# Fewer dummy matmuls in front, a layer norm's bias moved to VectorE, and a re-found instruction order

## The chip, the cores and the metric

The kernel runs on one core of one Trainium2 chip. The metric is the device time of one execution in microseconds (us). Beside the times there is one profiled execution, with a record of every instruction on five engines: TensorE (PE; PEld are its weight loads), VectorE (DVE), ScalarE (ACT), GpSimd (POOL) and SyncE (SP), which issues most DMAs.

## The reference, cut to what matters

```python
x = A_q                                             # [1, 2048, 512], bfloat16
xn = (x - mean(x)) / sqrt(var(x) + 1e-5)            # layer norm over the last axis
# branch A: a shift convolution (4 taps) of k, times v, then a long convolution over the sequence
k_shift = sum_t k_pad[:, t:t+S, :] * shift_k[:, 3 - t]
kv = k_shift * v
y = irfft(rfft(kv, 2S) * rfft(ssm_k, 2S))[:S] + kv * ssm_D
s = xn * y
# branch B: a gated feed-forward network, 512 -> 1792 -> 512
g = silu((gelu(xn @ w_gate) * (xn @ w_up)) @ w_down)
out = x + s * g
```

## The kernel before, in words

All 2048 rows are held as 16 tiles of 128 x 512 (`X`, normalized in `XN`), in four quarters q of four tiles. Branch B takes each quarter: layer norm (`ln`), transposition to `xnT`, then for each of 14 units (`unit`) gate and up matmuls (four of 128x512 each; the first two units of q 0 in halves of 256), gelu on ScalarE (`GE`), the product on VectorE (`HT`), and the down projection with `Wd` (`down`). Branch A does the long convolution as a two-stage Fourier transform by matmuls. Stage 1 of ssm_k (`stage1("H")`, line 938) writes eight results, which ScalarE evicts into four buffers that lie in unused halves of `XN` and `X`; VectorE adds two halves (line 947), and ScalarE's queue stores each to DRAM as `ZH`. A buffer is free again when its store has landed. They are loaded back as `BH` for stage 2 (32x512 matmuls, line 1010). k and v go the same way (`kshift` on VectorE, lines 987 to 995; `ZK`, `BK`); the product of the spectra (`spectrum`), the inverse (`ZI`, `BI`) and the last stage (line 1248) follow.

All loads go through SyncE's queue, in the order of `ORDER`. The stores of `ZH` and `ZI` are issued by ScalarE, the rest by SyncE.

Every piece of work is a task with one or two engines that can do it, its estimated duration, and the buffers that it reads and writes. `SEQ` lists all tasks by number, in the order in which they are recorded; a "b" behind a number takes the second engine. `Sched.run` goes through that list, and gives buffers and PSUM banks out as they come free by its estimates, so the order and the estimates together set which buffer each task gets. The engines then run their own instructions strictly in the recorded order, with semaphores between them.

`warm_up` (line 684) records `N_WARM` matmuls of a zeroed tile ahead of all others. In `ln` each tile's mean and variance are found on VectorE (lines 832 and 833), the epsilon is added on VectorE (line 840), and GpSimd takes the power -0.5 (line 841). For q > 0 it also makes the bias that ScalarE's form of the norm needs (line 850), in two instructions (lines 845 and 846); VectorE's form of the norm (line 851) needs none. For q = 0 all this is done tile by tile, for the others once for four tiles.

The matmuls of all weights come from one helper (line 626), and many evictions from another (lines 617 to 620).

Of the kernel before, what the change touches and what calls it, by code (L numbers as in the profile page):

```python
# [7 lines left out]
FP32 = mybir.dt.float32  # L8
# [16 lines left out]
N_WARM = 18  # L25
ORDER = "x00 h0 x01 w0 D0 h1 w1 x1 h2 h3 s0 k0 w2 k1 k2 w3 d0 d1 v0 v1 k3 v2 v3 x2 x3"
SEQ = (
# [263 lines left out]
class Sched:  # L291
# [11 lines left out]
    SHARED, WAIT, TAKEN = 46000.0, 3300.0, 1400.0  # L303
# [43 lines left out]
    def run(self):  # L347
# [4 lines left out]
        for name in SEQ.split():  # L352
# [3 lines left out]
            for d in t.deps:  # L356
                base = max(base, d.end + d.lat + (self.SEM if not d.nbytes else (400.0 if d.eng == "loads" else self.HEDGE) if t.opts[0][0] == "PE" else self.SEM if d.eng == "loads" else self.HEDGE2))
# [12 lines left out]
            elif t.nbytes:  # L370
# [5 lines left out]
                if en < self.SHARED:  # L376
                    pipe = max(pipe, en + 1000.0) + t.nbytes / self.SHARE_BW
                    t.end = pipe + 1000.0 + self.WAIT
                else:
                    pipe = max(pipe, t.start + 780.0) + t.nbytes / self.DMA_BW  # L380
                    t.end = pipe + 760.0
# [22 lines left out]
def build_kernel(nc, A_q, A_k, A_v, A_shift_k, A_ssm_k, A_ssm_D, B_w_gate, B_w_up, B_w_down, out):  # L404
    with ExitStack() as es0:
# [262 lines left out]
        def pool_id():  # L668
            P(lambda h: h.memset(NHALF[:], -0.5), [R_nh])
            P(lambda h: h.tensor_scalar(ident[:], K32[:], 0.0, None, ALU.is_equal), [R_id], [R_K32])  # L670
# [664 lines left out]
```

## Time and profile before

| | us |
|---|---|
| median of 3 runs | 191.64 (191.61 to 192.41) |
| the profiled execution | 192.79 |
| its span, first to last record | 191.0 |
| TensorE busy | 184.2 (96%) |
| VectorE busy | 166.0 (87%) |
| ScalarE busy | 139.4 (73%) |
| GpSimd busy | 14.9 (8%) |

Busy times overlap between engines, and within TensorE successive matmuls overlap too, so a high busy share does not by itself say that an engine is the limit. The chain of waits is the page's answer to that: it goes back from the last instruction, at each step to what released it. A row of the timeline gives start, duration of the merged group, engine, line, operation and tiles, and in brackets the idle time ahead of it and what ended that.

### The profile page before, as it was taken

The page shows a single profiled execution, that of the slowest core. Times are in us where ns is not written, and L with a number is a line of the kernel's source. Part 1 is how long each engine was busy: PE and PEld are TensorE (multiplying, and loading weights), DVE is VectorE, ACT ScalarE, POOL GpSimd, SP SyncE. Part 2 cuts the span into 40 slices and gives each one's busy share as a digit, 9 for nine tenths or more (in the row PEclk, how much of TensorE's full clock was granted, in tenths as well). Part 3 has the DMA queues.
Part 4 walks back from the last instruction along what each step waited for, and adds up shares of the span by engine and source line. Part 5 has one row for each costly group of instructions (what it writes and reads, how often), then busy time and mean ns, then how long its engine had stood idle before and what let it go on. Part 6 is the DMA issues. An engine that isn't in the chain of part 4 may idle for free.

```text
span 191.0 us, 3537 instructions
## 1 busy us (share of the span) xinstructions
PE 184.2 (96%) x1381; PEld 79.7 (42%) x1392; DVE 166.0 (87%) x244; ACT 139.4 (73%) x188; POOL 14.9 (8%) x31
## 2 busy tenths in 40 slices
PE   7899999999999999999999999999999999999993
PEld 2576544444333343344443434334343444444442
DVE  6889999999899999998697999979889965448955
ACT  5457999883969677888799678878987644364752
POOL 5310940000000000032000000000000000000000
PEclk9999999999999999999999999999999999999999
DMA  5999999996969964676999996865821355935653
GB/s 172 330 383 331 355 373 374 403 404 126 317 258 287 272 204 178 228 257 213 341 250 238 319 309 228 277 246 203 286 91 58 110 168 169 375 106 189 262 220 110
DMA packets 36422, 47.84 MB, mean 250 GB/s; under 512 B 7347, under 2 KB 26039, under 8 KB 36406
## 3 DMA queue, kind: packets, MB, share of 16 engines
q1 hardware_dynamic: 29878, 39.23, 63.5%
q10 hardware_dynamic: 6528, 8.39, 12.5%
q8 instruction: 11, 0.18, 0.4%
q14 instruction: 5, 0.04, 0.1%
HBM read 27.39 MB, written 14.68 MB: 220 GB/s over the span
## 4 chain that ended last, share of the span: by engine, by line
PE 84%; DVE 11%; issue 2%; ACT 1%; ACTq 0%; DVEq 0%
PE psall L626 72%; PE psall L1010 5%; PE psall L930 2%; PE psall L1248 2%; DVE HT L1178 2%; DVE KAC L993 2%; DVE KTM L991 2%; DVE stats L832 1%; DVE KAC L987 1%; PE psall L938 1%; PE psall L896 1%; ACT GE L1175 1%; DVE HTr L620 1%; PE psall L872 1%; DVE XN L947 1%
## 5 line engine op out<-in xcount | busy, mean ns | idle before, releaser
L626 PE MATMUL psall<-xnT,Wu 128*128 128x512 bf16 (+1 forms) x232 | 55.7, 372 | 0.1
L626 PE MATMUL psall<-xnT,Wg 128*128 128x512 bf16 (+1 forms) x232 | 54.7, 372 | 0.7 <-ACT xnT L617 0.7
L626 PE MATMUL psall<-Wd,HT 128*128 128x512 bf16 (+2 forms) x227 | 51.0, 366 | 1.0 <-issue 0.8
L1178 DVE TENSOR_TENSOR HT<-psall,GE 128x512 bf16<-128x512 f32 x54 | 36.6, 682 | 6.4 <-PE psall L626 5.9
L1175 ACT ACTIVATE GE<-psall 128x512 bf16<-128x512 f32 x54 | 31.5, 607 | 10.4 <-PE psall L626 8.7
L626 PEld LDWEIGHTS psall<-Wd,HT 128*128 128x128 bf16 x238 | 21.5, 98 | 27.7 <-issue 4.6
L626 PEld LDWEIGHTS psall<-xnT,Wg 128*128 128x128 bf16 x232 | 21.5, 98 | 27.5 <-issue 2.1
L626 PEld LDWEIGHTS psall<-xnT,Wu 128*128 128x128 bf16 x232 | 21.4, 98 | 26.5 <-issue 3.0
L617 ACT ACTIVATE BO<-psall 128x1024 bf16<-128x1024 f32 x22 | 21.6, 1025 | 10.3 <-PE psall L1248 5.2
L1113 DVE TENSOR_TENSOR HSW<-KB,HSW 128x2048 bf16<-128x2048 bf16 x16 | 19.2, 1219 | 0.2
L617 ACT ACTIVATE AST<-psall 128x1024 bf16<-128x1024 f32 x14 | 14.3, 1024 | 4.7 <-PE psall L930 2.8
L617 ACT ACTIVATE HSW<-psall 128x1024 bf16<-128x1024 f32 x15 | 14.8, 1023 | 3.2 <-PE psall L1010 3.0
L617 ACT ACTIVATE KB<-psall 128x1024 bf16<-128x1024 f32 x14 | 13.9, 1038 | 2.7 <-PE psall L1010 2.7
L993 DVE TENSOR_TENSOR KAC<-KAC,KTM 128x2048 bf16<-128x2048 bf16 x12 | 14.5, 1212 | 0.0
L991 DVE TENSOR_TENSOR KTM<-KK,SKB 128x2048 bf16<-128x2048 bf16 x12 | 14.5, 1212 | 0.0
L1204 DVE SCALAR_TENSOR_TENSOR G<-G,psall 128x512 bf16<-128x512 bf16 x12 | 8.1, 682 | 4.1 <-ACT G L1202 4.1
L832 DVE BATCH_NORM_STATS2 stats<-X 128x6 f32<-128x512 bf16 x16 | 10.5, 681 | 0.7 <-DMA X<-in_A_q_dram 0.7
L617 ACT ACTIVATE XN<-psall 128x1024 bf16<-128x1024 f32 x10 | 10.2, 1023 | 1.1 <-PE psall L938 1.1
L841 POOL TENSOR_TENSOR mv<-mv,NHALF 128x1 f32<-128x1 f32 (+1 forms) x7 | 5.8, 828 | 66.0 <-DVE mv L840 66.0
L1136 DVE TENSOR_TENSOR HSW<-HSW 128x2048 bf16<-128x2048 bf16 x8 | 9.7, 1217 | 0.0
L1113 DVE TENSOR_TENSOR KB<-KB,HSW 128x2048 bf16<-128x2048 bf16 x8 | 9.6, 1217 | 0.0
L1202 ACT ACTIVATE G<-psall 128x512 bf16<-128x512 f32 x12 | 7.0, 596 | 3.2 <-PE psall L626 2.9
(85 smaller groups left out, 155.6 us busy)
## 6 DMA issues: line engine op xcount, KB each, us to landing
BH<-ZH SPq DMA_DIRECT2D x8, 512.0 KB, 5.4
HSW<-HSW SPq DMA_DIRECT2D x16, 256.0 KB, 4.3
BK<-ZK SPq DMA_DIRECT2D x8, 512.0 KB, 5.1
ZI<-BO ACTq DMA_DIRECT2D x16, 256.0 KB, 2.5
BI<-ZI SPq DMA_DIRECT2D x8, 512.0 KB, 4.6
ZK<-AST SPq DMA_DIRECT2D x7, 512.0 KB, 2.9
ZH<-XN ACTq DMA_DIRECT2D x5, 512.0 KB, 3.8
Hn<-in_A_ssm_k_dram SPq DMA_DIRECT2D x4, 512.0 KB, 7.4
```

The costliest lines, as they stand in the source:

```text
L617: return h.activation(o, i, ACTF.Copy, scale=scale)
L626: return h.matmul(o, lhsT=l, rhs=r, start=st, stop=sp)
L832: t_stats[t] = op([("DVE", 670.0)], lambda e, h, t=t: h.bn_stats(stats[:, t, :], X[:, t, :]), r=[bX[q][t % 4]], w=[bst[t]], rr=[R_X[t]], w ...
L991: op([("DVE", dur)], lambda e, h, j=j, m=m: h.tensor_tensor(KTM[:, m.slot, :, :], kk(j), sk(j), ALU.mult), r=need + [bSKB[j], a], w=[m], r ...
L993: op([("DVE", dur)], lambda e, h, m=m: h.tensor_tensor(KAC[:, a.slot, :, :], KAC[:, a.slot, :, :], KTM[:, m.slot, :, :], ALU.add), r=[m], ...
L1010: trk.op("PE", lambda h: h.matmul(ps(s, i)[b, :], lhsT=wt(col)[a, :], rhs=data(col)[a, :], start=n < 16, stop=n >= len(todo) - 16, tile_po ...
L1113: return hd.tensor_tensor(pair(KB, *(2 * DM * z for z in slots())) if to else x, k, x, ALU.mult)
L1136: return hd.tensor_tensor(x, x, y, ALU.add)
L1175: op([("ACT", act(512))], lambda e, h: h.activation(GE[:, g.slot, :], bank(pg), ACTF.Gelu_apprx_tanh), r=[pg], w=[g], rr=lambda: R_bank(pg ...
L1178: op([("DVE", dve(512, 1))], lambda e, h: h.tensor_tensor(HT[:, q % 2, m, :], bank(pu), GE[:, g.slot, :], ALU.mult), r=[pu, g], w=[bHT[q][m]],
L1202: op([("ACT", act(n))], lambda e, h, g=g, pc=pc: h.activation(g, pc(), ACTF.Tanh, scale=0.5), r=[p], w=[bt], rr=lambda p=p: R_bank(p), ww= ...
L1204: op([("DVE", dve(512, 1))], lambda e, h, g=g, pc=pc: h.scalar_tensor_tensor(out=g, in0=g, scalar=1.0, in1=pc(), op0=ALU.add, op1=ALU.mult ...
```

## The change

- `N_WARM` is 12 in place of 18.
- For q > 0 the bias is one VectorE instruction (mean x -1 x rstd) in place of a multiply and a negation on GpSimd. For q = 0 the epsilon may also be added by ScalarE, with a new constant tile `EPSC`; the new `SEQ` does so for two of the four tiles.
- The estimates in `Sched.run` are changed: a task of TensorE that depends on another of TensorE starts at that one's end without a margin; a store that begins between 31 and 46 us is taken to land behind the last load; the power for q > 0 is taken to last 2.5 us in place of 0.85, and ten of the dummies to run at 427 ns in place of seven.
- `SEQ` is new throughout. In the built program the first matmuls behind the dummies are both halves of ssm_k's first tile, then two tiles of `XN`; the first three ZH stores follow each other directly, the next three as well; and the last down projection ends with all fourteen 384-wide matmuls and then all fourteen 128-wide ones, where before four of the 128-wide ones came ahead of the last five of the 384-wide. The number of matmuls is otherwise the same.

```diff
-N_WARM = 18
+N_WARM = 12
...
 SEQ = (
-    "16 17 18 19 20 0 2 7 21 8 4 6 3 10 11 22 23 1 24 25 26 27 65 66 73 67 68 76 28 48 5 74 75 86 49 9 12 90 71 77 29 30 78 87 31 32 33 34 35 36 37 "
...
+    "2 3 16 0 7 17 18 19 20 21 1 10 8 22 9 11 23 24 25 65 66 12 4 6 48 67 26 5 73b 49 68 76 74 75 86 90 77 78 87 71 91b 27 28 29 30 72 82 83 69 70 "
...
-    SHARED, WAIT, TAKEN = 46000.0, 3300.0, 1400.0
+    EARLY, SHARED, WAIT, TAKEN = 31000.0, 46000.0, 3300.0, 1400.0
...
-                if en < self.SHARED:
+                if en < self.EARLY:
                     pipe = max(pipe, en + 1000.0) + t.nbytes / self.SHARE_BW
                     t.end = pipe + 1000.0 + self.WAIT
+                elif en < self.SHARED:
+                    pipe = max(pipe, t.start + 780.0) + t.nbytes / self.DMA_BW
+                    t.end = max(pipe + 760.0, 200.0 + max(l.end for l in order if l.eng == "loads"))
...
+            P(lambda h: h.memset(EPSC[:], LN_EPS), [R_ep])
...
-        t_warm = S.add([("PE", 7 * 427.0 + (N_WARM - 7) * 217.0)], warm_up, r=[bwarm], w=[warm])
+        t_warm = S.add([("PE", 10 * 427.0 + (N_WARM - 10) * 217.0)], warm_up, r=[bwarm], w=[warm])
...
-                t_var = op([("DVE", 180.0)], lambda e, hd, ts=ts: hd.tensor_scalar(mv[:, ts, 2:3], mv[:, ts, 1:2], LN_EPS, None, ALU.add), r=bm, w=[be], rr=rm, ww=rm)
-                t_pw = op([("POOL", 850.0 if q else 600.0)], lambda e, hd, ts=ts, n=n: hd.tensor_tensor(mv[:, ts, 3:4], mv[:, ts, 2:3], NHALF[:, 0:n, :], ALU.pow),
+                def var(e, hd, ts=ts):
+                    if e == "ACT":
+                        return hd.activation(mv[:, ts, 2:3], mv[:, ts, 1:2], ACTF.Identity, bias=EPSC[:, 0, :], scale=1.0)
+                    return hd.tensor_scalar(mv[:, ts, 2:3], mv[:, ts, 1:2], LN_EPS, None, ALU.add)
+                t_var = op([("DVE", 180.0)] + ([] if q else [("ACT", 240.0)]), var, r=[bconst, *bm], w=[be], rr=rm + [R_ep], ww=rm)
+                t_pw = op([("POOL", 2500.0 if q else 600.0)], lambda e, hd, ts=ts, n=n: hd.tensor_tensor(mv[:, ts, 3:4], mv[:, ts, 2:3], NHALF[:, 0:n, :], ALU.pow),
                           r=[bconst, be] + bm, w=[b], rr=rm + [R_nh], ww=rm)
                 bn = B(f"nb{q}_{h}")
                 if q:
-                    op([("POOL", 800.0)], lambda e, hd, ts=ts: hd.tensor_tensor(NB_[:, ts, :], mv[:, ts, 0:1], mv[:, ts, 3:4], ALU.mult), r=[b], w=[bn], rr=rm, ww=R_nb[ts])
-                    op([("POOL", 500.0)], lambda e, hd, ts=ts: hd.tensor_scalar(NB_[:, ts, :], NB_[:, ts, :], -1.0, None, ALU.mult), r=[bn], w=[bn], rr=R_nb[ts], ww=R_nb[ts])
+                    op([("DVE", 200.0)], lambda e, hd, ts=ts: hd.scalar_tensor_tensor(out=NB_[:, ts, :], in0=mv[:, ts, 0:1], scalar=-1.0, in1=mv[:, ts, 3:4], op0=ALU.mult, op1=ALU.mult), r=[b], w=[bn], rr=rm, ww=R_nb[ts])
```

More of the change, by code (lines that the diff above doesn't have):

```diff
@@ L356, in run @@
             for d in t.deps:
-                base = max(base, d.end + d.lat + (self.SEM if not d.nbytes else (400.0 if d.eng == "loads" else self.HEDGE) if t.opts[0][0] == "PE" else self.SEM if d.eng == "loads" else self.HEDGE2))
+                base = max(base, d.end if d.eng == "PE" == t.opts[0][0] else d.end + d.lat + (self.SEM if not d.nbytes else (400.0 if d.eng == "loads" else self.HEDGE) if t.opts[0][0] == "PE" else self.SEM if d.eng == "loads" else self.HEDGE2))
             for b in t.w:
@@ L440, in build_kernel @@
         NHALF = new("NHALF", [128, 4, 1], FP32)
+        EPSC = new("EPSC", [128, 1, 1], FP32)
         NB_ = new("NB_", [128, NT, 1], FP32)
@@ L530, in build_kernel @@
         R_nh = res("NHALF", NHALF[:])
+        R_ep = res("EPSC", EPSC[:])
         R_nb = [res(f"nb{t}", NB_[:, t, :]) for t in range(NT)]
```

41 rows, old and new, of the table SEQ are left out of this document.

## The prediction

> **What bounds the kernel now.** I read the page first, then the chain of waits, then the busy time by stretches.
>
> ```profile
> span 191.0 us, 3537 instructions
> ...
> PE 184.2 (96%) x1381; PEld 79.7 (42%) x1392; DVE 166.0 (87%) x244; ACT 139.4 (73%) x188; POOL 14.9 (8%) x31
> ...
> PE 84%; DVE 11%; issue 2%; ACT 1%; ACTq 0%; DVEq 0%
> ```
>
> TensorE is busy 184.2 of 191.0 us and carries 84% of the chain that ended last; VectorE carries 11%. So the time is the sum of TensorE's instructions plus the few places where it stands still, and only what shortens that sum or those places counts. The profiled execution took 192.79 us with this span of 191.0; the median of the three timed runs is 191.64. I carry differences from the span over to the median.
>
> ```profile
> 14.94 2.39 DVE stats L832 x4
> ...
> 36.65 2.76 PE psall L626 x12
> ...
> 156.68 11.82 PE psall L626 x54
> ```
> ```profile
> 20.00:30.00 10.00, 10.00 (x55) 4.57 (x52) 10.00 (x15) 9.97 (x14) 5.80 (x6) 1.00 1.07 366
> 30.00:40.00 10.00, 9.95 (x56) 3.92 (x55) 10.00 (x13) 8.90 (x14) 0.00 (x0) 1.00 1.06 397
> ```
>
> The first fence has pieces of the chain (start, us), the second the busy time by stretch: TensorE, weight loads, VectorE, ScalarE, GpSimd. From 14.94 to 36.65 nearly all pieces are VectorE's, which is busy 10.00 of 10.00 us twice running; TensorE has work there too, but cannot get ahead of VectorE. After 36.65 the chain is nearly all TensorE's. The 54 matmuls in 11.82 us give 0.219 us each.
>
> **The dummies and the front.** These rows of the timeline (start, us, engine, line) are the start of the kernel.
>
> ```profile
> 1.21 6.33 PE L626 MATMUL psall<-AST 128*128 128x512 bf16 x18 [1.21 <-DVE AST L680]
> ...
> 4.15 0.69 DVE L832 BATCH_NORM_STATS2 stats<-X 128x6 f32<-128x512 bf16 x1 [0.19 <-DMA X<-in_A_q_dram]
> ...
> 5.40 0.57 POOL L841 TENSOR_TENSOR mv<-mv,NHALF 128x1 f32<-128x1 f32 x1 [1.90 <-DVE mv L840]
> ...
> 5.71 0.20 ACT L732 ACTIVATE COLS<-COLS 128x1 f32<-128x1 f32 x1
> ...
> 6.17 0.40 DVE L851 TENSOR_SCALAR XN<-X,mv 128x512 bf16<-128x512 bf16 x1
> ...
> 7.04 0.69 DVE L832 BATCH_NORM_STATS2 stats<-X 128x6 f32<-128x512 bf16 x1 [0.46 <-DMA X<-in_A_q_dram]
> ...
> 7.37 0.61 PE L896 MATMUL psall<-ident,Hn 128*128 128x128 f32 x4
> ...
> 7.82 0.39 PE L872 MATMUL psall<-ident,XN 128*128 128x128 bf16 x4
> ...
> 8.04 0.66 PE L896 MATMUL psall<-ident,Hn 128*128 128x128 f32 x4
> 8.24 1.32 ACT L617 ACTIVATE xnT<-psall 128x512 bf16<-128x512 bf16 x2 [2.33 <-PE psall L872]
> ...
> 9.61 0.61 PE L626 MATMUL psall<-xnT,Wg 128*128 128x256 bf16 x4 [0.69 <-ACT xnT L617]
> ...
> 10.93 0.61 PE L872 MATMUL psall<-ident,XN 128*128 128x128 bf16 x8
> ...
> 13.19 2.75 PE L626 MATMUL psall<-xnT,Wg 128*128 128x512 bf16 x12
> ```
>
> Six dummies of 0.219 us are 1.31 us, so TensorE is free at 7.37 - 1.31 = 6.06. The first tile of ssm_k lies between the two halves of x in the same queue, so it lands between 4.15 and 7.04 (no row has its landing; I take "before 6.06", and lose up to 1.0 us of the gain if not). The new order puts both its halves first: eight transposes of (7.82 - 7.37) / 4 = 0.11 us, until 6.95. Then TensorE needs normalized rows. That chain starts at 4.15 whatever the dummies do, and the change makes its first link later: the variance's epsilon goes from VectorE (0.15 us, line 840) to ScalarE, which is free only after the 5.71 row, at about 5.9. With 0.2 us for it the power begins near 6.2, not 5.40; norm follows 0.2 us after the power's end (5.40 + 0.57 to 6.17), so near 7.0; the transposes come at 7.3 to 7.5 and the second tile's 0.6 later. One eviction is now VectorE's, behind a statistics instruction of 0.69, so both are done by 8.6 to 9.0 instead of 9.61 less the wake-up. The second half of x (7.04) gets its statistics after the norms, so the third and fourth transposes come near 10.4 and 11.5, and TensorE idles before both, which it did not in the one batch at 10.93. After eight more ssm_k transposes it reaches the first 512-wide gate matmuls at 12.4 to 12.8 instead of 13.19, with four more transposes done (0.44 us) and eight fewer 256-wide matmuls of (10.93 - 9.61) / 12 = 0.11 us (0.88 us). Net gain: 13.19 - 12.4 + 0.44 - 0.88 = 0.35 at best by this chain, nothing at 12.8. I take 0.2, with bounds of 0 and, if no wait of the chain were left, 1.31 + 0.69 = 2.0. What covered the removed dummies was thus mostly waiting for x, and that waiting stays.
>
> The granted clock is the second thing that the dummies do: 18 in 6.33 us is far more than 18 x 0.219 = 3.9 us, so (6.33 - 3.94) / 0.219 = about 11 of them ran at half speed. Twelve end about when full speed came. The Trainium skill, "TensorE: Matmul & The Clock Gate", section "Part 1: The HAM clock gate", says that the clock is released after a busy window of about 3.4 us that runs freely, and falls back after an idle window as long; by it the release may come earlier or later from run to run, and the front's gaps, each under 1 us, would not undo it. The trace agrees in part: full speed came some 4.8 us after the first dummy (11 x 0.43), and behind the 0.69 us gap at 9.61 the matmuls still take 0.11 each. The same page, section "A second HAM failure mode: psum-queue depth-cycling", says that frequent short idling can let the clock swing; that is a rival below.
>
> **The late stores.** This is where TensorE stands still in the body.
>
> ```profile
> 36.08 0.37 ACTq L599 DMA_DIRECT2D ZH<-X  x1
> ...
> 43.02 0.61 PE L938 MATMUL psall<-HTr,F 64*128 64x512 bf16 x4
> 43.56 1.90 PE L626 MATMUL psall<-xnT,Wg 128*128 128x512 bf16 x8
> ...
> 46.51 2.08 ACT L617 ACTIVATE X<-psall 128x1024 bf16<-128x1024 f32 x2 [2.98 <-DMA ZH<-X]
> ...
> 49.28 0.39 PE L938 MATMUL psall<-HTr,F 64*128 64x512 bf16 x1
> ...
> 50.11 0.60 PE L938 MATMUL psall<-HTr,F 64*128 64x512 bf16 x3 [0.45 <-ACT GE L1175]
> ```
> ```profile
> ZH<-XN ACTq DMA_DIRECT2D x5, 512.0 KB, 3.8
> ```
>
> The store issued at 36.08 landed at about 46.5, over 10 us later, against a median of 3.8 for its kind: loads were ahead of it. ScalarE stood 2.98 us for its buffer, the gelu evictions queued behind, and TensorE, which wanted their PSUM bank, started the rest of a group at 50.11 that began at 49.28: 0.83 us, where an undisturbed group (43.02 to 43.56) takes 0.54 in all. In the new order three stores stand in a row early, and the fourth stands behind the second quarter's xnT evictions, with two more. Those evictions ran just before the 43.02 row, so these stores fall near the end of the loads; the 46.51 row shows when those were done. Between the fourth store's issue and the eviction that needs its buffer ScalarE has two more issues (0.37 each), a gelu (0.6) and an XN eviction (1.0): 2.3 us. With 3.8 us to land it waits 1.5. In the trace 2.98 cost 0.83, so 2.15 would have cost nothing: 0.83 comes back, with 0.65 to spare. Bounds: the whole 0.83, and far below nothing if the store is slow (the rival).
>
> **The bias.** Three times, GpSimd's multiply and negation become one VectorE instruction.
>
> ```profile
> 22.05 1.02 POOL L841 TENSOR_TENSOR mv<-mv,NHALF 128x4 f32<-128x4 f32 x1
> ...
> 23.15 2.49 POOL L845 TENSOR_TENSOR NB__68<-mv 128x4 f32<-128x4 f32 x1
> ...
> 25.73 0.24 POOL L846 TENSOR_SCALAR NB__68<-NB__68 128x4 f32<-128x4 f32 x1
> ...
> 89.73 1.03 POOL L841 TENSOR_TENSOR mv<-mv,NHALF 128x4 f32<-128x4 f32 x1 [4.07 <-DVE mv L840]
> ```
> ```profile
> L840 DVE TENSOR_SCALAR mv<-mv 128x4 f32<-128x4 f32 x3 | 0.6, 202 | 0.0
> L850 ACT ACTIVATE XN<-X,NB__68,mv x9: 803/819/873, 29.0 to 97.7; 128x512 bf16<-128x512 bf16 x9
> 90.00:100.00 10.00, 9.81 (x87) 4.08 (x88) 8.37 (x9) 8.51 (x11) 1.19 (x3) 1.00 1.05 300
> ```
> GpSimd is done at 25.97, and ScalarE's first norm that reads the bias stands at 29.0, so the 2.7 us that GpSimd saves release nobody. VectorE gets an instruction like the 0.202 us one of line 840. The one for the second quarter of x falls into the stretch where VectorE is full, so it costs its 0.1 to 0.2 us on the path; the others fall where VectorE has 1.6 us free in ten. The instruction waits for the power: in the second quarter nine VectorE instructions stand between, in the last none, so there VectorE stops for about 1.03 + 0.3 us, with the norms and a KB eviction behind it. TensorE is then in matmuls of Wd whose inputs are long made; without that cover it would cost up to 1.3 us.
>
> **The rest of the order and the end.** Counted in the order of the two builds, there are the same matmuls and the same 44 groups of tiled ones among the full ones, so TensorE's sum is otherwise unchanged.
>
> ```profile
> 182.78 5.00 PE L626 MATMUL psall<-Wd,HT 128*128 128x512 bf16 x34
> ...
> 187.27 0.84 ACT L1210 ACTIVATE G<-psall 128x384 bf16<-128x384 f32 x2 [0.44 <-PE psall L626]
> ...
> 188.71 0.23 DVE L1213 TENSOR_TENSOR G<-G,X 128x128 bf16<-128x128 bf16 x1
> ```
> ScalarE's eviction at 187.27 starts a chain that ends the kernel: VectorE works off the 384 columns before the last 128. Now all fourteen 128-wide matmuls stand behind the last 384-wide one, before only ten, so the 384 columns are ready 4 x 0.219 / 4 = 0.2 us earlier against TensorE's end: 0.2 us gained (0 to 0.3). New small waits on a full VectorE between 20 and 50 us no row of before can show; I allow 0.2 in all, the bias's share included (0 to 2).
>
> Sum: -0.2 (front) - 0.83 (store) - 0.2 (end) + 0.2 = -1.03: span 190.0, profiled execution 191.8, median 191.64 - 1.03 = **190.6**. A measurement of this kernel can tell about 0.5%, 0.96 us, from no change; the forecast lies just beyond it.
>
> **Rivals.** *VectorE keeps what is won.* It is full from 14.94 to 36.65, and its first piece there waits for x's next load, not for TensorE. Then the front's gain is gone, the re-found order has small waits of its own in place of the 0.83, and only the end's 0.2 is left: about 191.4. For it: the two rows of 10.00. Against: the 0.83 lies after that stretch. Chance 0.33.
>
> *ScalarE waits for the fourth store.* Its place is the X eviction behind the three stores near 45 us. It decides from a landing of 2.3 + 2.15 = 4.45 us: each us more is a us of TensorE. Half way between 3.8 and the 10.4 of the trace, 7.1, it loses 2.65: 193.25. At 6.45 us the time is 192.6, slower by 0.5%. For it: three stores share the queue, and the loads may end later, since three stores now go early. Against: it is issued when the loads are nearly done. Chance 0.20.
>
> *The clock.* With twelve dummies and gaps behind them full speed comes late or is lost until about 12 us. TensorE's work from 6.06 to 12.4 is 16 transposes of ssm_k and 16 matmuls of 0.11 each and 16 transposes of x of (8.04 - 7.82) / 4 = 0.055, together 4.4 us; at half speed 4.4 more, of which about 2.0 disappear in the gaps: 190.6 + 2.4 = 193.0. Against it: the gaps are short. Chance 0.05.
>
> **How the numbers follow.** The forecast has 0.42: 190.6, and down to 191.64 - 2.0 = 189.6 if the front's waits vanish. So faster 0.42; within 0.5% 0.33; slower 0.20 + 0.05 = 0.25. The forecast's own range is 189.8 to 190.7. The range for 8 in 10 takes in the first rival, the clock and the store up to a landing of 7.05 us: 189.8 to 193.2 leaves out about 0.05 below and 0.12 above.
>
> **What would show it.** Right: the first eight transposes near 6.1, first gate matmuls before 9.1, first 512-wide ones at 12.4 to 12.8; none of the eight groups of ssm_k's first stage (line 938, now 946) over 0.6 us; ScalarE's wait for a ZH store under 2.15 us; the last VectorE row 0.2 us closer to TensorE's end. Wrong: a TensorE gap of over 0.5 us between 40 and 60, a ZH store of over 5 us issued after 44, dummies or transposes at half speed behind 6.1, or VectorE idle behind the power while TensorE waits for it.

## The result, and the profile after

The changed kernel takes 191.03 us (median of seven runs, six of them 190.94 to 191.25). Two disturbed runs, one of 475.59 here and one of 196.06 of the kernel with the third store late, are left out of the ratios; the medians hold all runs. The kernel before, run beside it on the same chip, took 192.3 (191.47 to 193.03). The ratio is 0.994 (95% interval 0.9915 to 0.9965), that is 0.6% or 1.15 us faster. As the control of a later group it gave 191.40 and a ratio of 0.9955 (0.9932 to 0.9978). The forecast was a fall of 1.03 us or 0.54%, between the two. The forecast's 190.6 itself lies 0.4 to 0.8 us below the medians: it stood on a median of three runs for the kernel before, and in the five groups here that kernel has medians of 191.94 to 192.36 and single runs from 191.25 to 193.81. That spread turns out to be half of the story.

The page of the profiled execution (190.94 us), first lines and the shares of the chain of waits:

```profile
span 189.1 us, 3534 instructions
...
PE 183.5 (97%) x1386; PEld 78.4 (41%) x1386; DVE 168.4 (89%) x250; ACT 136.1 (72%) x185; POOL 12.7 (7%) x26
...
PE 92%; DVE 3%; ACT 2%; POOL 1%; issue 0%
```

By the two pages TensorE's busy time is 0.7 us less than before, the span 1.9 us. That does not mean that most of the fall is standing still that went. The page before has 1381 matmuls to 1392 weight loads, this one 1386 of each, so eleven matmul records of before are missing. They are all of the down projection (its group before, then after):

```profile
L626 PE MATMUL psall<-Wd,HT 128*128 128x512 bf16 (+2 forms) x227 | 51.0, 366 | 1.0 <-issue 0.8
L630 PE MATMUL psall<-Wd,HT 128*128 128x512 bf16 (+2 forms) x238 | 51.6, 367 | 0.0
```

Each missing record leaves a gap of 0.05 to 0.16 us that looks like idle time, 1.2 us in all. With them TensorE was busy for about 185.4 us before, and its busy time fell by about as much as the span; the dummies alone last 4.17 us in place of 6.33. TensorE now carries 92% of the chain where it carried 84%; VectorE's 11% became 3%. Of these 1.9 us, 0.7 to 1.0 are this pair of executions (192.79 and 190.94, where the two ratios give 0.9 to 1.15). TensorE's rows of the timeline at the front (start, us, engine, line):

```profile
1.21 4.17 PE L630 MATMUL psall<-AST 128*128 128x512 bf16 x12 [1.21 <-DVE AST L685]
5.55 1.14 PE L904 MATMUL psall<-ident,Hn 128*128 128x128 f32 x8 [0.17 <-DMA Hn<-in_A_ssm_k_dram]
6.70 0.93 PE L880 MATMUL psall<-ident,XN 128*128 128x128 bf16 x8
8.15 1.05 PE L630 MATMUL psall<-xnT,Wg 128*128 128x256 bf16 x8 [0.53 <-DVE xnT L624]
...
12.18 2.11 PE L630 MATMUL psall<-xnT,Wg 128*128 128x512 bf16 x11
```

The dummies are done by 5.4, TensorE then waits 0.17 us for ssm_k's first tile, and the first 512-wide gate matmul stands at 12.18, ahead of the forecast's 12.4 to 12.8. Around the late stores (first three rows ScalarE's queue and ScalarE, then TensorE, then the busy time by stretch in the columns of the prediction's second fence):

```profile
28.40 0.52 ACTq L603 DMA_DIRECT2D ZH<-XN  x1
...
43.95 0.37 ACTq L603 DMA_DIRECT2D ZH<-X  x1
...
48.25 2.08 ACT L621 ACTIVATE X<-psall 128x1024 bf16<-128x1024 f32 x2 [0.92 <-PE psall L946]
```
```profile
47.61 0.61 PE L946 MATMUL psall<-HTr,F 64*128 64x512 bf16 x4
```
```profile
20.00:30.00 10.00, 10.00 (x53) 4.40 (x51) 10.00 (x19) 8.64 (x11) 4.58 (x4) 1.00 1.07 365
30.00:40.00 10.00, 10.00 (x54) 3.88 (x53) 10.00 (x12) 9.94 (x16) 0.00 (x0) 1.00 1.07 400
40.00:50.00 10.00, 10.00 (x59) 4.39 (x58) 10.00 (x13) 7.58 (x10) 0.00 (x0) 1.00 1.06 337
```

The third ZH store is issued at 28.40 where before it was at 36.08, and the fourth at 43.95 landed within 3.9 us. The eviction that needs its buffer (48.25) waited for TensorE, not for a store. The sixth store, issued at 44.88, took 5.5 us, which the prediction names as a sign of being wrong; nothing waited for it. No group of ssm_k's first stage is broken up any more. VectorE is full from 20 us on, now to 60, and yet TensorE is busy 10.00 of 10.00: the small new waits that I had allowed for do not show. The end of the kernel, from TensorE and VectorE:

```profile
179.91 6.25 PE L630 MATMUL psall<-Wd,HT 128*128 128x512 bf16 x42
...
186.85 0.23 DVE L1221 TENSOR_TENSOR G<-G,X 128x128 bf16<-128x128 bf16 x1
```

TensorE ends at 179.91 + 6.25 = 186.16, and the last VectorE row starts 0.69 us later. Before it was 188.71 - (182.78 + 5.00) = 0.93.

### The profile page after: what moved, and what is told of

It reads as the page before. It is cut to its first block, busy times and chain, and to the rows that moved or that the text cites. A ratio compares the mean times of both kernels' runs of the same rounds, so it can differ in the third digit from the quotient of the medians.

```text
span 189.1 us, 3534 instructions
## 1 busy us (share of the span) xinstructions
PE 183.5 (97%) x1386; PEld 78.4 (41%) x1386; DVE 168.4 (89%) x250; ACT 136.1 (72%) x185; POOL 12.7 (7%) x26
## 4 chain that ended last, share of the span: by engine, by line
PE 92%; DVE 3%; ACT 2%; POOL 1%; issue 0%
PE psall L630 78%; PE psall L1018 6%; PE psall L946 2%; PE psall L938 2%; PE psall L1256 2%; PE psall L904 2%; POOL mv L850 1%; PE psall L880 1%; ACT L737 1%; DVE stats L837 1%; DVE XN L859 0%; DVE G L1221 0%; DVE G L1220 0%; DVE C L709 0%; ACT G L1218 0%
## 5 line engine op out<-in xcount | busy, mean ns | idle before, releaser
L630 PE MATMUL psall<-xnT,Wg 128*128 128x512 bf16 (+1 forms) x232 | 55.3, 372 | 0.5 <-DVE xnT L624 0.5
L630 PE MATMUL psall<-Wd,HT 128*128 128x512 bf16 (+2 forms) x238 | 51.6, 367 | 0.0
L1186 DVE TENSOR_TENSOR HT<-psall,GE 128x512 bf16<-128x512 f32 x54 | 36.1, 680 | 6.5 <-PE psall L630 6.2
L621 ACT ACTIVATE BO<-psall 128x1024 bf16<-128x1024 f32 x19 | 19.0, 1023 | 7.7 <-PE psall L1018 4.0
L621 ACT ACTIVATE HSW<-psall 128x1024 bf16<-128x1024 f32 x16 | 15.8, 1031 | 3.5 <-PE psall L1018 3.5
L621 ACT ACTIVATE AST<-psall 128x1024 bf16<-128x1024 f32 x12 | 12.3, 1023 | 1.4 <-PE psall L938 1.2
L850 POOL TENSOR_TENSOR mv<-mv,NHALF 128x1 f32<-128x1 f32 (+1 forms) x7 | 7.1, 1021 | 67.4 <-DVE mv L848 64.7
L621 ACT ACTIVATE X<-psall 128x1024 bf16<-128x1024 f32 x8 | 8.2, 1023 | 1.0 <-PE psall L946 0.9
L621 ACT ACTIVATE XN<-psall 128x1024 bf16<-128x1024 f32 x8 | 8.1, 1024 | 1.0 <-PE psall L946 0.9
```

What stands on the lines that cost most here:

```text
L621: return h.activation(o, i, ACTF.Copy, scale=scale)
L630: return h.matmul(o, lhsT=l, rhs=r, start=st, stop=sp)
L850: t_pw = op([("POOL", 2500.0 if q else 600.0)], lambda e, hd, ts=ts, n=n: hd.tensor_tensor(mv[:, ts, 3:4], mv[:, ts, 2:3], NHALF[:, 0:n, : ...
L1186: op([("DVE", dve(512, 1))], lambda e, h: h.tensor_tensor(HT[:, q % 2, m, :], bank(pu), GE[:, g.slot, :], ALU.mult), r=[pu, g], w=[bHT[q][m]],
```

## The experiments

Most of these move one instruction or change one number. Where an instruction is moved, buffers and PSUM banks are still handed out by the old list, and only the order of recording changes, so nothing else differs. Where the number of dummies changes, the estimate of their time is held at that of the kernel that was edited (a line that the diffs leave out), so that the order stays as it is. All but one are timed in five rounds beside the kernel before, in three groups and a last single run. The groups ran on different chips, so numbers of different groups are compared by their ratios. A ratio is not the quotient of the two medians beside it; where they differ, its interval says what can be told.

| experiment | median, us | median of before beside it | ratio to before (95%) |
|---|---|---|---|
| changed, 18 dummies | 192.23 | 192.09 | 1.0004 (0.9983 to 1.0026) |
| before, 12 dummies | 191.75 | 192.09 | 1.0003 (0.9977 to 1.0028) |
| before, third store early | 191.77 | 192.09 | 0.9990 (0.9968 to 1.0011) |
| changed, third store late | 192.52 | 192.09 | 1.0031 (1.0008 to 1.0053) |
| changed (control) | 191.40 | 191.94 | 0.9955 (0.9932 to 0.9978) |
| changed, end as before | 191.59 | 191.94 | 0.9973 (0.9947 to 0.9999) |
| changed, bias on GpSimd | 191.46 | 191.94 | 0.9975 (0.9943 to 1.0008) |
| changed, front wait filled | 191.20 | 191.94 | 0.9957 (0.9933 to 0.9980) |
| before with three edits | 191.41 | 192.36 | 0.9953 (0.9936 to 0.9970) |
| changed, 8 dummies | 191.25 | 192.36 | 0.9958 (0.9935 to 0.9981) |
| a version meant to be faster | 191.05 | 192.28 | 0.9947 (0.9927 to 0.9967) |

### The dummies back in the changed kernel

```diff
-N_WARM = 12
+N_WARM = 18
```

> The changed kernel with 18 dummies again, all else in its order. Theory (the dummies hid a wait for x): TensorE is free about 6 x 0.22 = 1.3 us later, near 6.5, but in the changed kernel it stands still for 0.17 + 0.30 + 0.69 + 0.78 = 1.9 us between 6.4 and 11.0, so most of that is swallowed: 0 to 0.4 us slower than the changed kernel, 191.0 to 191.4, first 512-wide gate matmuls at 12.2 to 12.6. Rival (the dummies stood in the way): the whole 1.3 us comes back, 192.3, first 512-wide ones at 13.5.

This and the control bracket the dummies. TensorE's and VectorE's rows with 18 dummies, then with 12 (the control):

```profile
1.20 6.03 PE L630 MATMUL psall<-AST 128*128 128x512 bf16 x18 [1.20 <-DVE AST L685]
...
8.60 0.42 DVE L624 COPY xnT<-psall 128x512 bf16<-128x512 bf16 x1 [0.82 <-PE psall L880]
...
13.10 2.11 PE L630 MATMUL psall<-xnT,Wg 128*128 128x512 bf16 x11
```
```profile
1.20 5.12 PE L630 MATMUL psall<-AST 128*128 128x512 bf16 x12 [1.20 <-DVE AST L685]
...
7.69 0.42 DVE L624 COPY xnT<-psall 128x512 bf16<-128x512 bf16 x1
...
12.20 2.76 PE L630 MATMUL psall<-xnT,Wg 128*128 128x512 bf16 x16
```

The rival is nearly right: the first 512-wide matmul comes 0.90 us later, and the ratio is 0.0049 higher than the control's, 0.94 us (by the two intervals 0.3 to 1.5). The rows say why the waits did not swallow it. In the new order VectorE evicts one of the two transposed tiles. With TensorE late that eviction starts at 8.60 in place of 7.69, VectorE waits 0.82 us for it, and everything behind it in VectorE's queue (the second half's statistics, then its norms) moves by the same 0.91. The wait that I took for a wait on x was a wait on VectorE, and VectorE waits for TensorE. A smaller delay the wait for x does swallow: in the control TensorE begins ssm_k's transposes 0.61 us later than in the changed kernel's first trace (6.16 against 5.55), and the first 512-wide matmul comes only 0.02 us later.

### The dummies alone in the kernel before

```diff
-N_WARM = 18
+N_WARM = 12
```

> The kernel before with 12 dummies and nothing else changed. Theory (the dummies hid a wait for x): its 0.85 us gap near 8.7 takes up what is cut; 0 to 0.4 us faster than before, and the stall of 0.83 us at 49.3 stays. Rival (the dummies stood in the way): 1.3 us faster. Second rival (the clock needs the dummies): matmuls at half speed behind 6 us, 1 us or more slower.

```profile
1.21 4.07 PE L626 MATMUL psall<-AST 128*128 128x512 bf16 x12 [1.21 <-DVE AST L680]
...
12.30 1.89 PE L626 MATMUL psall<-xnT,Wg 128*128 128x512 bf16 x8
...
29.18 0.81 ACT L850 ACTIVATE XN<-X,NB__68,mv 128x512 bf16<-128x512 bf16 x1 [0.90 <-POOL NB__68 L846]
...
44.73 2.08 ACT L617 ACTIVATE X<-psall 128x1024 bf16<-128x1024 f32 x2 [1.97 <-PE psall L626]
...
48.52 0.61 PE L938 MATMUL psall<-HTr,F 64*128 64x512 bf16 x4
```

In the trace the front is 0.51 us earlier than in the next experiment, which has the same front with 18 dummies and as early a clock (12.30 against 12.81). Yet the ratio shows no change (1.0003, at most 0.2% faster), though the median is 0.34 us lower. The times lie in two groups, 191.20 to 191.84 (seven) and 192.56 to 192.97 (five). The profiled execution, 191.20 us, is of the first: in it the third ZH store landed at 44.65, and the group at 48.52 is whole.

This trace also shows the bias: GpSimd's pair ended at 29.14 here, ScalarE's first norm waited 0.90 us for it, and at 33.07 TensorE stood still for 0.20 us behind an eviction that follows those norms on ScalarE. So the bias on GpSimd is not free in every execution.

### The third store early in the kernel before

```diff
-        order = S.run()
+        order = S.run(); order.remove(S.tasks[103]); order.insert(order.index(S.tasks[108]) + 1, S.tasks[103])
```

> The kernel before with one instruction moved: the third ZH store is issued right behind the second (at 28 to 30 us) in place of 36.1. Theory (the store wait was worth its 0.83 us): it lands near 37 to 39, ScalarE's X eviction near 43.5 no longer waits 2.98 us for it, all eight groups of ssm_k's first stage take 0.54, and the time falls by 0.8 us. Rival (VectorE keeps what is won): the wait goes and the time stays within 0.2 us. Second rival (the store delays the loads): the 512 KB push the later loads back by about 1.3 us and a new wait of up to that shows on a load, time unchanged or up to 1.3 us slower.

```profile
1.21 5.46 PE L626 MATMUL psall<-AST 128*128 128x512 bf16 x18 [1.21 <-DVE AST L680]
...
12.81 1.46 PE L626 MATMUL psall<-xnT,Wg 128*128 128x512 bf16 x6
...
43.26 2.08 ACT L617 ACTIVATE X<-psall 128x1024 bf16<-128x1024 f32 x2
...
48.88 0.61 PE L938 MATMUL psall<-HTr,F 64*128 64x512 bf16 x4
```

The wait is gone as the theory has it: issued at 29.29 the store landed at 37.39, ScalarE's eviction at 43.26 waits for nothing, and the last load lands at 46.1, no later than before (46.3). But the ratio says 0.1% (at most 0.3%; the median is 0.32 us lower), not the 0.83 us or 0.43% of the prediction's trace.

### The third store late in the changed kernel

```diff
-        order = S.run()
+        order = S.run(); order.remove(S.tasks[108]); order.insert(order.index(S.tasks[403]) + 1, S.tasks[108])
```

> The changed kernel with one instruction moved: the third ZH store is issued near 37 us in place of 28.4. Theory: it lands behind the loads, near 46.4 as in the kernel before, and ScalarE's XN eviction, which started at 43.9 in the changed kernel, waits for it until then: 2.5 us on ScalarE, of which 0.8 us (the price of 2.98 before) to 2.5 us reach TensorE; 191.8 to 193.5. Rival (VectorE or the order hides it): within 0.2 us of the changed kernel, 191.0.

```profile
35.74 0.37 ACTq L603 DMA_DIRECT2D ZH<-XN  x1
...
44.96 1.02 ACT L621 ACTIVATE XN<-psall 128x1024 bf16<-128x1024 f32 x1 [1.58 <-PE psall L630]
...
47.63 0.39 PE L946 MATMUL psall<-HTr,F 64*128 64x512 bf16 x1
48.54 0.60 PE L946 MATMUL psall<-HTr,F 64*128 64x512 bf16 x3 [0.53 <-ACT XN L621]
```

Shown: one store moved by 7 us brings the stall back. It landed at 44.88, and the eviction started at 44.96. (The row names TensorE as the releaser, but those matmuls had been done for long; the store came last.) TensorE breaks off the group at 47.63 and resumes at 48.54, 0.91 us. The span is 1.0 us over that of the changed kernel, and the ratio is 0.0076 over the control's, 1.5 us (by the two intervals 0.8 to 2.1); the single executions reach from 191.79 to 193.39.

### A second trace of the kernel before

> The kernel before once more, unaltered, for a second trace of it. Its timed executions lie in two groups, near 191.6 and near 192.8 us. Theory (the third ZH store's landing is a race with the loads): in a short execution it lands before about 45.5 us and the group of four at 49 us takes 0.54; in a long one it lands near 46.4 and the group takes about 1.3. Rival (the two groups are the clock's release alone): the stall of 0.8 us is there in both, and the dummies at half speed are 6 in the short one and 11 or more in the long one.

```profile
1.21 6.71 PE L626 MATMUL psall<-AST 128*128 128x512 bf16 x18 [1.21 <-DVE AST L680]
...
13.57 0.59 PE L626 MATMUL psall<-xnT,Wg 128*128 128x512 bf16 x2
...
46.20 2.08 ACT L617 ACTIVATE X<-psall 128x1024 bf16<-128x1024 f32 x2 [2.37 <-PE psall L626]
...
49.57 0.83 PE L938 MATMUL psall<-HTr,F 64*128 64x512 bf16 x4
50.33 2.76 PE L626 MATMUL psall<-Wd,HT 128*128 128x512 bf16 x12
```

This execution took 192.48 us, and both theories have a part in it. Full speed came late: (6.71 - 18 x 0.219) / 0.219 gives about 13 dummies at half speed, against 11 in the prediction's trace and 7 in the one just above. So the first 512-wide matmul stands at 13.57, against 13.19 and 12.81. The store landed at 46.11, and the group lasts from 49.57 to 50.33 = 0.76 us, a stall of only 0.22. ScalarE waited for this store for 2.98 us in the prediction's trace, 2.37 here and 1.97 with 12 dummies, and TensorE stood 0.83, 0.22 and 0 us: the prediction's 2.15 us that cost nothing fit all three. (Two of the rows name TensorE as the releaser, but the store had landed 0.08 to 0.09 us before each eviction.) Now compare the ends: from the eviction behind the store to the first matmul behind the group it is 50.33 - 46.20 = 4.13 us here, and in the prediction's rows, where the next down matmuls follow the group at 50.65, it is 50.65 - 46.51 = 4.14. The store's landing, not the front, sets when TensorE goes on. A front that is 0.38 us earlier (the prediction's trace) only stands 0.6 us longer, since the store also landed 0.3 later.

In the four traces with a late store it landed right behind one of the last two loads: at 44.65 and 44.88, behind the last but one (44.5 and 44.6), where it was issued at 35.55 and 35.74; at 46.43 and 46.11, behind the last (46.3 and 46.1), where it was issued at 36.08 and 36.45. So TensorE seems to be let go at one of two times some 1.5 us apart, and an earlier front may just reach the first. Four traces do not prove it.

### The three edits in the old order

12 dummies, the third store early, and the end's four 128-wide matmuls behind the last 384-wide ones, in the kernel before:

```diff
-N_WARM = 18
+N_WARM = 12
...
-        order = S.run()
+        order = S.run(); order.remove(S.tasks[103]); order.insert(order.index(S.tasks[108]) + 1, S.tasks[103]); order.remove(S.tasks[761]); order.insert(order.index(S.tasks[756]) + 1, S.tasks[761])
```

> The old order with three small edits and nothing else of the change: 12 dummies, the third ZH store right behind the second, and the end's four 128-wide matmuls behind the last 384-wide ones. Theory (the gain is these three, not the re-found order as such): the profiles so far give 0.3 to 0.5 us for the dummies in the old order, up to 0.83 us for the store in those executions that have the stall, 0.25 us for the end; so about 0.9 us below the kernel before, ratio 0.995, the changed kernel's own. Rival (the re-found order carries it): ratio 0.998 or more.

```profile
1.20 5.30 PE L626 MATMUL psall<-AST 128*128 128x512 bf16 x12 [1.20 <-DVE AST L680]
...
12.54 2.75 PE L626 MATMUL psall<-xnT,Wg 128*128 128x512 bf16 x12
```

The ratio is 0.9953 (0.9936 to 0.9970) and the median 191.41, the changed kernel's own. As far as 0.2% can be told, three small edits are thus worth as much as the whole re-found order with its bias instruction; the rival (0.998 or more) falls outside the interval. Here all twelve dummies ran at half speed ((5.30 - 12 x 0.219) / 0.219 = 12.2), and the first 512-wide matmul is still only 0.24 us later than with seven (12.54 against 12.30). With 18 dummies nearly the same difference of the clock (7 and 13) was 13.57 - 12.81 = 0.76.

Alone the first edit gave 1.0003 and the second 0.9990; with the end's 0.2 us (measured below) that would make about 0.998, were they to add up. Together they give 0.9953. The times do not show that this is more than the sum: the difference of 0.003 has an uncertainty of 0.004 by the intervals, and by the medians (0.34, 0.32 and 0.2 us alone, 0.95 together) the edits nearly add up. The traces show how it could be more: with the store late, an earlier front ends at a gate, the store's landing; with the store early, nothing holds it. No long execution of the kernel with the dummies alone was traced, so for that kernel this is argued: with a landing at 46.1 to 46.4 its group, which ended at 49.05, would end near 50.3 to 50.65, 1.3 to 1.6 us later, and its two groups of times lie 1.2 us apart.

### The control, the end, the bias and the filled wait

The control is the changed kernel unaltered:

> The changed kernel once more, unaltered, as the control of this group and for its spread. Theory A (with twelve dummies the front waits for ssm_k's first tile, landed at 5.42 us, and not for the dummies, so the clock's release may come earlier or later without effect): nearly all executions within 0.5 us, 190.9 to 191.4. Rival (the tight first measurement was chance, its executions fell on an early release): a spread of 1.5 us as in the kernel before, median near 191.7.

It has 11 dummies at half speed ((5.12 - 12 x 0.219) / 0.219) where the first trace had 7, and the first 512-wide matmul moves by 0.02 us (12.20 against 12.18). Theory A holds there. The spread is 1.0 us (191.03 to 192.00), not the 0.5 I expected, nor the 2.5 of the kernel before in the same group (191.31 to 193.81). In this trace 0.3 us were lost near 17.3 us, in the transposes of ssm_k's last tiles, whose last load landed at 17.50 where in the first trace it did at 16.75.

The end as before:

```diff
-        order = S.run()
+        order = S.run(); order.remove(S.tasks[758]); order.insert(order.index(S.tasks[752]) + 1, S.tasks[758])
```

> The changed kernel with the end's order of before: four of the last 128-wide matmuls go ahead of the last five 384-wide ones. Theory: ScalarE's 384-wide eviction starts 0.2 us later against TensorE's end, so the last VectorE row stands 0.2 us later against it; 0.2 us slower than the control. Rival (VectorE's queue of the last 1024-wide adds sets the end, not the 384 columns): no difference in the last row.

TensorE's last row and VectorE's, with the old end and in the control:

```profile
180.00 6.25 PE L630 MATMUL psall<-Wd,HT 128*128 128x512 bf16 x41
...
187.17 0.22 DVE L1221 TENSOR_TENSOR G<-G,X 128x128 bf16<-128x128 bf16 x1
```
```profile
180.25 6.25 PE L630 MATMUL psall<-Wd,HT 128*128 128x512 bf16 x41
...
187.20 0.23 DVE L1221 TENSOR_TENSOR G<-G,X 128x128 bf16<-128x128 bf16 x1
```

0.92 us from TensorE's end to the last row, against 0.70: the 0.2 us are there, and the medians (191.59 and 191.40) agree, though the intervals of the ratios overlap.

The bias on GpSimd:

```diff
-                    op([("DVE", 200.0)], lambda e, hd, ts=ts: hd.scalar_tensor_tensor(...), r=[b], w=[bn], ...)
+                    S.add([("DVE", 200.0)], lambda e, ts=ts, rm=rm: (trk.op("POOL", ... ALU.mult ...), trk.op("POOL", ... -1.0 ...)), r=[b], w=[bn])
```

> The changed kernel with the bias of the three later quarters back on GpSimd, two instructions each, all else in its order. Theory (the bias is near nothing either way): ScalarE's first norm of the second quarter stood at 30.56 behind other work, GpSimd's pair (2.7 us in the kernel before) begins near 23 and ends before that; VectorE, full from 20 to 60 us, is 0.2 us shorter; within 0.2 us of the control. Rival (the power ends so late that the pair's 2.7 us hold up ScalarE's norms, or the pair slows VectorE while both run): up to 2 us slower, with TensorE waiting between 30 and 45 us.

```profile
25.25 4.31 POOL L854 TENSOR_TENSOR NB__69<-mv 128x4 f32<-128x4 f32 x1
29.64 0.24 POOL L854 TENSOR_SCALAR NB__69<-NB__69 128x4 f32<-128x4 f32 x1
...
30.87 1.51 ACT L858 ACTIVATE XN<-X,NB__69,mv 128x512 bf16<-128x512 bf16 x2
```

No difference that can be told: the medians are 191.46 and 191.40, and the ratio's interval is wide, with one run of 193.77 among the twelve. But the cover was thinner than I had it: GpSimd's multiply took 4.31 us here against 2.49 in the prediction's rows, and its pair was done at 29.88, 1.0 us ahead of ScalarE's first use.

The wait at 10.1 us filled with half of the next tile's transposes:

```diff
-        order = S.run()
+        order = S.run(); order.remove(S.tasks[52]); order.insert(order.index(S.tasks[350]) + 1, S.tasks[52])
```

> A version meant to be faster: the changed kernel with the first four transposes of ssm_k's second tile moved into TensorE's wait at 10.1 to 11.0 us, ahead of the transposes of the third tile of XN. Its PSUM bank is free from 10.43 us, the tile landed at 9.93. Theory (what the front saves is kept to the end): the first 512-wide gate matmul starts near 11.9 in place of 12.18, and everything behind it by the same 0.3 us earlier; 0.3 us faster than the control. Rival (VectorE, full from 20 us, takes it back): the front starts earlier, the end doesn't.

```profile
12.08 2.77 PE L630 MATMUL psall<-xnT,Wg 128*128 128x512 bf16 x16
...
19.62 1.05 DVE L918 TENSOR_TENSOR HTr<-HTr,Drow 1x512 bf16<-1x512 bf16 x1
...
21.36 0.60 PE L946 MATMUL psall<-HTr,F 64*128 64x512 bf16 x4 [0.18 <-DVE HT L1186]
```

The front came earlier, by 0.1 us against the changed kernel although ssm_k's tile was 0.16 later, but at 21.36 TensorE waits for VectorE, 0.19 us later than in the changed kernel (21.17). The ratio is the control's; the median is 0.2 lower, within what can be told.

### Eight dummies, and a faster version

```diff
-N_WARM = 12
+N_WARM = 8
```

> The changed kernel with 8 dummies. Theory (ssm_k's first tile, landed at 5.4 us, is the front's bound, not the dummies): the dummies end by 4.7 us at the latest, the first transposes still start at 5.5, and the time is the changed kernel's, ratio 0.995 to 0.996; an execution in which the clock is released late gains up to 0.3 us. Rival (the clock needs them): with TensorE idle for 1 us ahead of 5.5 us the release comes later, transposes and the first gate matmuls run at half speed, and the time is 1 us or more longer.

```profile
5.67 1.13 PE L904 MATMUL psall<-ident,Hn 128*128 128x128 f32 x8 [0.88 <-DMA Hn<-in_A_ssm_k_dram]
...
12.19 2.76 PE L630 MATMUL psall<-xnT,Wg 128*128 128x512 bf16 x16
```

The theory holds: TensorE waits 0.88 us for the tile in place of 0.17, and the front is where it was. Ten runs are 190.95 to 192.29; four of them are above 191.7, so late executions were not cured.

The last version joins 10 dummies, the filled wait, and VectorE's one-row addition moved to 35 us:

```diff
-N_WARM = 12
+N_WARM = 10
...
-        order = S.run()
+        order = S.run(); order.remove(S.tasks[52]); order.insert(order.index(S.tasks[350]) + 1, S.tasks[52]); order.remove(S.tasks[64]); order.insert(order.index(S.tasks[143]) + 1, S.tasks[64])
```

> A version meant to beat both: the changed kernel with 10 dummies, with four transposes of ssm_k's second tile in TensorE's wait at 10.1 us, and with VectorE's one-row addition of D to ssm_k (0.72 to 1.11 us at 19.7 us in the traces, just ahead of a group of ssm_k's first stage that waited 0.1 to 0.25 us more for VectorE) moved to about 35 us, nine microseconds ahead of its only reader. Theory (TensorE's front waits are kept to the end): 0.3 us from the filled wait, 0.1 to 0.3 from the addition, up to 0.3 in executions where the clock comes late; ratio to the kernel before 0.993 to 0.994. Rival (VectorE is full from 20 to 60 us, so what leaves one place waits at another): the changed kernel's 0.9955.

```profile
11.94 2.34 PE L630 MATMUL psall<-xnT,Wg 128*128 128x512 bf16 x12
...
33.98 0.72 DVE L918 TENSOR_TENSOR HTr<-HTr,Drow 1x512 bf16<-1x512 bf16 x1
```

Median 191.05, ratio 0.9947 (0.9927 to 0.9967). That beats the kernel before; against the changed kernel (0.9955) the intervals overlap. What it does have is the narrowest spread: twelve runs from 191.02 to 191.37. In its trace the front is 0.24 us earlier (11.94), and 0.3 us are lost again between the third and the fourth of ssm_k's groups, so part of the rival is true as well.

## Why the prediction was right, point by point

**The sum** was right: -1.03 us or 0.54% forecast, 0.45% to 0.6% measured, and the mechanism (a front wait, a store wait, the end) is the one that the three edits reproduce. Two of its terms were mis-sized in opposite directions, the front too small and the store too large; that these errors nearly cancel is luck.

**The front, 0.2 us.** The step that failed is "what covered the removed dummies was thus mostly waiting for x, and that waiting stays". That waiting swallows about 0.6 us of lateness and no more; putting six dummies back cost 0.94 us. The second failing is that one execution's clock was taken for the kernel's. In the prediction's own tally (0.44 us of extra work done, 0.88 not yet) the changed kernel's 12.18 and 12.20 count as 12.62 and 12.64. The old order's front stood at 12.81 (the kernel with only the store moved), 13.19 and 13.57 in three traces with 7, 11 and 13 slow dummies. So the front's gain is 0.2, 0.6 and 0.9 us, by how late the clock comes; 0.2 is its lower end. Of the other steps, two held: the tile of ssm_k landed before 6.06 (at 5.42), and the first gate matmuls came before 9.1 (8.15; the expected "8.6 to 9.0" was too late since ScalarE was free 0.6 us earlier). Of the two waits expected at the third and the fourth tile only the second came (0.62 us at 11.00); the third tile's transposes stand at 9.55 with next to none. So the chain from x was shorter than forecast, and the first 512-wide matmul came at 12.18, ahead of the best case of 12.4.

**The clock.** The Trainium skill, "TensorE: Matmul & The Clock Gate", section "Part 1: The HAM clock gate", gives 6, 11 or 14 slow matmuls for one and the same kernel, by the phase of a window that runs freely. The traces agree that the count varies: 7, 11 and 13 of 18, and 7, 11 and 12 of 12; that the phase of a window does it, no run here shows. The Trainium skill adds that the ramp costs less than 1% of a typical span and that one should not fit to a specific count. The 0.76 us here are 0.4% of the span, and still the difference between 12.81 and 13.57 is most of what the change is about. The rival in which full speed is lost behind twelve dummies did not come up, not with eight either.

**The store, 0.83 us.** The mechanism was right, and the late store in the changed kernel brought 0.91 us back. The size was that of one execution: in three traces of the old order with the late store it is 0.83, 0.22 and 0, with landings at 46.43, 46.11 and 44.65. Removed alone it was worth 0.2 us (0.9990, at most 0.6 us). In the new order the margin asked for, a landing under 4.45 us, was met with 3.9.

**The end, 0.2 us**: 0.93 to 0.69 in the traces, and 0.22 by the experiment. **The small waits, 0.2 us**: none in the changed kernel's trace, where no wait of TensorE shows behind 13 us; 0.2 to 0.3 in those of some experiments. **The bias**: VectorE waits for the power as predicted, 1.1 us in all against 1.3, with TensorE at 10.00 of 10.00. That GpSimd's saving releases nobody held in the prediction's trace but not with 12 dummies in the old order, where TensorE lost 0.2 us behind it. The row of the groups:

```profile
L854 DVE SCALAR_TENSOR_TENSOR NB__69<-mv 128x4 f32<-128x4 f32 x3 | 0.5, 156 | 1.1 <-POOL mv L850 1.1
```

**The rivals.** "VectorE keeps what is won" was wrong: 0.9 us at the front were 0.9 at the end. "ScalarE waits for the fourth store" was wrong in the changed kernel, but the price that it names was shown when the third store was moved. It was also close: in the traces with the filled wait and of the faster version this eviction did wait for the fourth store, which took 4.5 and 4.3 us, at the margin of 4.45, and TensorE shows no wait behind it. Open remains what makes some executions of the changed kernel 0.5 to 1 us longer than others; a fourth store that takes a little longer is a candidate that no run here tests.

## What to carry to other kernels

Ask of each wait that is to swallow a delay whether the waited-for engine has the delayed one ahead of it in its own queue; if so, the wait moves along and swallows nothing. A wait that ends with a transfer hides what is won ahead of it. Here two edits that could each not be told from nothing gave, with a third of 0.1%, 0.5% together: try such edits together before dropping either. Count matmuls against weight loads before reading a busy share, since missing records look like idle time. And look at the spread of the runs before believing one trace's stall: a kernel whose times lie in two groups may have a race in it, and one trace shows only one outcome of it.

## What the runs showed of the hardware

GpSimd's first 128x4 instructions take very different times: the power 1.01 to 3.82 us and the multiply 0.20 to 4.31, while VectorE is full; the later ones take 1.0 to 1.4 and 0.20. VectorE's addition of one row of 512, near 20 us while GpSimd copies, took 0.72 to 1.17 us. The Trainium skill, "SBUF — State Buffer", section "SBUF: two separate sides", says that a VectorE instruction with two SBUF inputs and a GpSimd instruction that reads SBUF hold a shared pair of ports against each other for the whole instruction. No run here settles whether that is the cause: moved to 33.98 us, where GpSimd does nothing, the addition took 0.72, but it took 0.72 beside the copies in the changed kernel as well. Of the power and the multiply no run here took VectorE's work away.

A store of 512 KB takes longer to land while loads are under way: 6.3 to 10.4 us from an issue between 26 and 36.5 us, and 2.8 to 4.5 us for the fourth of the new order, issued near 44, when the loads are nearly done. The landing of the late store differs by 1.8 us between executions (44.65 to 46.43).
